# A prologue rewritten: filters by GpSimd's queue, one load for both middle matrices, x first, a shorter weight conversion

## The chip, the cores and the metric

The kernel runs on one core of a Trainium2 chip. The metric is the device time of one execution in microseconds, taken as the median of three runs. A profile of one execution shows every instruction of TensorE (PE), VectorE (DVE), ScalarE (ACT), GpSimd (POOL) and the queue of SyncE (SP), and every DMA packet.

## The reference

```
X = rfft(x, axis=1)                      # x: 8 x 3008 x 256, float32
y = irfft(X * (filt_r + 1j*filt_i), n=3008, axis=1)   # filters: 1505 x 256
t = y.reshape(24064, 256)
h = t @ w_in                             # 256 x 2048, stored as float64
out = (h - tanh(h)) @ w_out              # 2048 x 256, stored as float64
```

A circular convolution along the sequence comes first, then a feed-forward block with the activation h - tanh(h).

## The kernel before, in words

The length 3008 is 64 x 47, so each Fourier transform is done in two steps by matrix products. `first` applies the 64-point step to x and writes the result to the scratch tensor `ct1` in memory. `middle` reads `ct1` back (`load_a2`), applies the 47-point step with a matrix per frequency group (`f2`, giving `pz`), multiplies by the filters (`uv`, `zs`), applies the inverse 47-point step (`g3`, giving `pe`), and writes `ct2`. `last` reads `ct2` (`load_e2`), applies the inverse 64-point step and leaves the transposed tokens in `ut`. `up`, `shrink` and `down` are the feed-forward block, with seven products in place of eight blocks (the sums that this needs are GpSimd's `combine`). The batches are handled in five units: one batch, three pairs, one batch.

The first unit has a stage of its own, the prologue (L738 to L912). Nothing of the feed-forward block can run until its tokens are there, so it runs alone: `first0` for three pieces of x, then a loop over j = 0..15 with two frequencies each. Four frequencies (two values of j) share one load of `a2`, of the matrices and of the filters; the text calls such a group c, from 0 to 7. In this stage DVE computes `uv` and `zs` straight from PSUM (L899, L900), ACT copies the filters to the other 64 partitions (`double_filters`, L815) and builds `gx`, a turned copy of `g3` (`turned`, L823, L824), and `back0` makes `pe` and stores it to `ct2` (L879).

Beside it the weights are converted. They lie in memory as 64-bit floats and are loaded as pairs of 32-bit words (`raw`, L193, 512 KB a piece). `converted` turns one piece into float32 with integer operations on DVE and two on ACT (L200 to L219); every second piece is followed by four subtractions on GpSimd (L261 to L264) for the seven-product scheme. Ten pieces are converted in the prologue, six more (`late`) while the first unit's feed-forward block runs. In the same time the filters are copied from the inputs to the scratch tensor `filt_d` in the layout that the other units read (`filters_d`, 52 transfers from memory to memory, L791).

Order: in the prologue every instruction stands in the order of the program text, per engine. Transfers that are not part of it (the late weight pieces, the copies to `filt_d`) are put by the scheduler wherever it finds room on SP's queue. In the feed-forward stage PE, ACT, DVE and GpSimd are in the order of the text, with SP left to the scheduler. A queue works through its instructions in order, and one that waits holds up those behind it. The transfers that SP and ACT issue share eight completion counters in turn, so that an issue also waits until the transfer eight places earlier, on either queue, has landed; GpSimd's transfers have eight counters of their own.

Buffers of the prologue: `big` is a ring of five tiles of 8 KB a partition, used in turn by a tile of zeros, three pieces of x and the filters of each c; `a1` (three tiles) holds results of `first0`; the tiles of the conversion have rings of two.

Of the kernel before, what the change touches and what calls it, by code (L numbers as in the profile page):

```python
# [9 lines left out]
F32 = mybir.dt.float32  # L10
I32 = mybir.dt.int32
I64 = mybir.dt.int64
U8 = mybir.dt.uint8
AF = mybir.ActivationFunctionType
ALU = mybir.AluOpType
# [5 lines left out]
BATCH, SEQ, DM = 8, 3008, 256  # L21
NQ, NR = 64, 47
NK = NQ // 2
R2 = 2 * NR

RP = 48
RP2 = 2 * RP
LO = (NR + 1) // 2
HI = NR - LO
IM = 64  # L30
# [7 lines left out]
UNITS = [(0,), (1, 2), (3, 4), (5, 6), (7,)]  # L38
# [25 lines left out]
def _consts():  # L64
# [11 lines left out]
    wf1 = np.zeros((2, 128, 64, 2))  # L76
# [50 lines left out]
    for b in range(2):  # L127
        s2[64 * b:64 * b + 64, 64 * b:64 * b + 64] = s

    return [np.ascontiguousarray(v, dtype=np.float32) for v in (  # L130
        wf1,
        np.pad(f2w.transpose(1, 0, 2).reshape(R2, NK * 128), ((0, 2), (0, 0))),
        np.pad(g.transpose(1, 0, 2).reshape(IM + NR, NK, 2, NR),
               ((0, 1), (0, 0), (0, 0), (0, 1))).reshape(IM + RP, NK * RP2),
        s2)]


@with_exitstack
def kernel(
# [8 lines left out]
):  # L148
    nc = tc.nc
    V, G, ACT = nc.vector, nc.gpsimd, nc.scalar  # L150
    wf1_d, f2_d, g_d, s2_d = (
        nc.inline_tensor(v, name=n).ap() for v, n in zip(_consts(), ("wf1", "f2", "g", "s2")))


    ct1 = [nc.dram_tensor(f"ct1_{p}", (RP, 64 * len(bs), DM), F32, kind="Internal")
# [8 lines left out]
    def dram(t, off, dims):  # L164
        return bass.AP(tensor=t, offset=off, ap=[list(d) for d in dims])
# [21 lines left out]
    def converted(tiles, src, dsts, queue):  # L187

        n = src.shape[-1] * (src.shape[1] if len(src.shape) == 3 else 1)
        t = tiles("raw", I64, n)
        queue.dma_start(t if len(src.shape) == 2 else  # L193
                        t.rearrange("p (h n) -> p h n", h=src.shape[1]), src)
        yield
        words = t.bitcast(I32).rearrange("p (n w) -> p n w", w=2)
        lo, hi = words[:, :, 0], words[:, :, 1]
        it, lt, pt, st = (tiles(k, I32, n) for k in ("it", "lt", "pt", "st"))
        ft = tiles("ft", F32, n)
        V.tensor_scalar(out=it, in0=hi, scalar1=0xFFFFF, scalar2=None, op0=ALU.bitwise_and)  # L200
        ACT.activation(ft, it, AF.Identity, bias=1.0, scale=2.0 ** -20)

        V.tensor_scalar(out=pt, in0=hi, scalar1=20, scalar2=0x7FF,
                        op0=ALU.logical_shift_right, op1=ALU.bitwise_and)
        ACT.activation(pt, pt, AF.Relu, bias=exp_b)
        V.tensor_scalar(out=lt, in0=lo, scalar1=8, scalar2=None, op0=ALU.logical_shift_right)
        V.tensor_scalar(out=st, in0=hi, scalar1=-2 ** 31, scalar2=None, op0=ALU.bitwise_and)
        yield
        V.scalar_tensor_tensor(out=ft, in0=lt, scalar=2.0 ** -44, in1=ft,
                               op0=ALU.mult, op1=ALU.add)  # L210
        V.tensor_scalar_min(pt, pt, 255.0)
        V.scalar_tensor_tensor(out=pt, in0=pt, scalar=23, in1=st,
                               op0=ALU.logical_shift_left, op1=ALU.bitwise_or)
        pt = pt.bitcast(F32)
        for cols, dst, sign in dsts:
            f, p = ft[:, cols], pt[:, cols]
            if len(dst.shape) == 3:
                f, p = (v.rearrange("p (h n) -> p h n", h=dst.shape[1]) for v in (f, p))
            V.scalar_tensor_tensor(out=dst, in0=f, scalar=sign, in1=p, op0=ALU.mult, op1=ALU.mult)  # L219
        yield  # L220
# [46 lines left out]
    def halves(p, r, n):  # L267

        return [(h, slice(64 * h, 64 * h + 64), r + HALF * h, min(n, NR - r - HALF * h))
                for h in range(2) if r + HALF * h < NR]  # L270
# [42 lines left out]
                        a1[rows, 0:n_h, :])  # L313
            yield

    def load_slots(p, j):

        f2 = tr.tile([RP2, 4, 128], F32, tag="f2", bufs=2, name="f2")
        g3 = tr.tile([IM + RP, 4, RP2], F32, tag="g3", bufs=2, name="g3")
        nc.sync.dma_start(f2, f2_d[:, 4 * j * 128:4 * (j + 1) * 128])  # L320
        nc.sync.dma_start(g3, g_d[:, 4 * j * RP2:4 * (j + 1) * RP2])
        return f2, g3

    def load_a2(p, j, filters=True):

# [15 lines left out]
    def middle(p, z):  # L341
# [3 lines left out]
        n = NK // per  # L345
        w = BD // per
        a2 = {0: load_a2(p, 0)}
        mats = {0: load_slots(p, 0)}
        waiting = []
        yield  # L350

# [13 lines left out]
        for j in range(n):  # L365
# [1 line left out]
                a2[j // 2 + 1] = load_a2(p, j // 2 + 1)  # L367
            k4 = per * j // 4
            if per * j % 4 == 0 and k4 + 1 < NK // 4:
                mats[k4 + 1] = load_slots(p, k4 + 1)  # L370
            pz = z("pz", [128, per, w])
            at, ft = a2[j // 2] if j % 2 == 0 else a2.pop(j // 2)
            for i in range(per):
# [363 lines left out]
    with tc.tile_pool(name="tr", bufs=2) as tr:  # L737
        with tc.tile_pool(name="pro", bufs=1) as pro, \  # L738
# [2 lines left out]
            def z0(name, shape):  # L741
                return ps0.tile(shape, F32, tag="z", bufs=6, name=name)

            def big(shape, name):

                return pro.tile(shape, F32, tag="big", bufs=5, name=name)

            def load_x0(c):
                t = big([128, 8, DM], "x0")
                for _, rows, r, n in halves(0, 8 * c, 8):  # L750
                    nc.sync.dma_start(t[rows, 0:n, :],
                                      dram(x.tensor, r * DM, [[NR * DM, 64], [1, n * DM]]))
                return t

            def first0(xt, c):

                for i in range(2):
                    r = 8 * c + 4 * i
                    a1 = pro.tile([128, 4, DM], F32, tag="a1", bufs=3, name="a1")
                    parts = halves(0, r, 4)  # L760
                    m = parts[1][3]
                    for j in range(2):
# [17 lines left out]
            def filters_of(c, to=None):  # L780
# [4 lines left out]
                def put(row, m, v, i, n_s, src, off, dims):  # L785
                    if to is None:
                        dst = t[row:row + m, v, i:i + n_s, :]
                    else:
                        dst = dram(to, ((row * 2 + v) * NK + 4 * c + i) * DM,
                                   [[2 * NK * DM, m], [DM, n_s], [1, DM]])  # L790
                    nc.sync.dma_start(dst, dram(src.tensor, off, dims))  # L791

                if to is None:
                    t = big([128, 2, 4, DM], "filt")


                    G.memset(t[32:64], 0.0)
                    if n == 3:
                        G.memset(t[0:1, 1, 3], 0.0)
                for v, src in enumerate((filt_r, filt_i)):  # L800
# [23 lines left out]
                ACT.mul(t[IM:IM + RP], g3[0:RP], -1.0)  # L824

            def tiles0(k, dtype, n):
                return pro.tile([128, n], dtype, tag=k, bufs=3 if k == "raw" else 2, name=k)

            with tc.manual_schedule():
                nc.sync.dma_start(wf1, wf1_d)  # L830
                V.memset(near_b, B)
                V.memset(exp_b, -896.0)
                zero = big([128, 8 * DM], "zero")
                G.memset(zero, 0.0)
                gx = [pro.tile([IM + RP, 4, RP2], F32, name=f"gx{k}") for k in range(2)]
                for t in gx:
                    G.memset(t[32:64], 0.0)
                xs = [load_x0(0)]
                ws = weights(tiles0, range(5), 3)
                next(ws)  # L840
                xs += [load_x0(1), load_x0(2)]


                for p, bs in enumerate(UNITS):
                    G.dma_start(
                        dram(ct1[p], NR * 64 * len(bs) * DM, [[DM, 64 * len(bs)], [1, DM]]),
                        zero[0:64 * len(bs), 0:DM])
                row = 2 * NK * DM
                G.dma_start(dram(filt_d, RP * row, [[8 * DM, 128], [1, 8 * DM]]), zero)
                G.dma_start(dram(filt_d, NR * row, [[DM // 2, 128], [1, DM // 2]]),  # L850
                            zero[:, 0:DM // 2])
                G.dma_start(dram(filt_d, (NK + NK - 1) * DM, [[DM, 1], [1, DM]]), zero[0:1, 0:DM])
                G.dma_start(s2, s2_d)
                mats = {0: load_slots(0, 0)}
                fts = {0: filters_of(0)}
                for c in range(3):
                    for k, _ in enumerate(first0(xs[c], c)):
                        if k % 2 == 0:
                            next(ws)
                    if c == 0:  # L860
                        fts[1] = filters_of(1)
                a2 = {0: load_a2(0, 0, False)}
                double_filters(fts[0], 0)
                turned(mats[0][1], gx[0])
                waiting = []
# [16 lines left out]
                for j in range(NK // 2):  # L882
                    c = j // 2
                    if j % 2 == 0 and c + 1 < NK // 4:
                        a2[c + 1] = load_a2(0, c + 1, False)
                        mats[c + 1] = load_slots(0, c + 1)
                        if c + 2 < NK // 4:
                            fts[c + 2] = filters_of(c + 2)
                    pz = z0("pz", [128, 2, DM])
                    for i in range(2):  # L890
# [24 lines left out]
        with tc.tile_pool(name="dn", bufs=2) as dn, \  # L915
# [5 lines left out]

            def tiles1(k, dtype, n):

                tag = {"raw": "ft", "it": "uv", "lt": "zs", "pt": "a2", "st": "e1", "ft": "f2"}[k]
                return tr.tile([128, n], dtype, tag=tag, bufs=2, name=k)

            def filters_d():
                for c in range(NK // 4):
                    filters_of(c, filt_d)
                    yield  # L930
# [121 lines left out]
```

## Time and profile before

| | us |
|---|---|
| runs (median of three) | 2888.24 (2887.48 to 2889.82) |
| the profiled execution | 2892.35 |
| its span, first to last instruction | 2890.6 |
| prologue, to the first `pu` product | 129.4 |
| of it, to the first `pz` product | 48.7 |
| of it, the sixteen steps j, to the last `pe` | 73.0 |
| feed-forward block and other units | 2761 |

The profiled execution has 1.75 us outside its span. A page of the profile gives shares for the whole span; stages are read from busy time by window, waits by window and the order of instructions in time. In a list of waits, a line names the engine and line that waited, what released it, the total, the number of times and the longest.

### The profile page before, as it was taken

What the parts mean: (1) busy time and instruction counts of PE and PEld (TensorE: products, weight loads), DVE (VectorE), ACT (ScalarE), POOL (GpSimd) and SP (SyncE); (2) the same over time, 40 slices, a digit from 0 to 9 for tenths busy, and PEclk for the clock granted to TensorE, in tenths of its full rate; (3) what the DMA queues carried; (4) which work ended last, traced back from release to release, by engine and by line L of the source; (5) the groups of instructions that cost most, each with busy time, mean ns of one, the idle gap of its engine ahead of it and who ended that gap; (6) DMA issues with size and microseconds to landing.
All of it is one profiled execution on the core that took longest, in us unless ns stands there. A gap on an engine that the chain in (4) does not pass through costs nothing.

```text
span 2890.6 us, 36570 instructions
## 1 busy us (share of the span) xinstructions
PE 2746.8 (95%) x12474; PEld 2277.0 (79%) x12474; DVE 1998.8 (69%) x2230; ACT 1871.7 (65%) x2460; POOL 1736.7 (60%) x1338
## 2 busy tenths in 40 slices
PE   4789999999999999999999999999999999999996
PEld 2567777888878787888877887888888888888885
DVE  4585666766776677766776777767677767777765
ACT  4465666666667666666667766666666666666663
POOL 3245777544677767644576777654476666555544
PEclk8799999999999999999999999999999999999998
DMA  8655443233223322222223233312123222110100
GB/s 245 180 161 137 114 102 98 79 85 93 58 69 72 85 68 62 59 85 82 72 72 75 65 74 80 72 38 65 41 52 79 47 56 49 31 28 16 22 8 16
DMA packets 332377, 216.15 MB, mean 75 GB/s; under 512 B 229139, under 2 KB 285878, under 8 KB 331734
## 3 DMA queue, kind: packets, MB, share of 16 engines
q1 hardware_dynamic: 279316, 162.20, 23.4%
q10 hardware_dynamic: 52418, 49.82, 5.7%
q8 instruction: 100, 1.64, 0.2%
q0 software_dynamic: 448, 1.71, 0.1%
q14 instruction: 95, 0.78, 0.1%
HBM read 137.50 MB, written 79.17 MB: 75 GB/s over the span
## 4 chain that ended last, share of the span: by engine, by line
PE 66%; ACT 9%; DVE 9%; POOL 5%; issue 4%; DMA 4%; SPq 2%; ACTq 1%; DVEq 0%; POOLq 0%
PE o L576 26%; PE x L469 17%; PE z L469 7%; PE y L469 5%; PE pe L357 3%; DVE h L530 3%; PE pu L433 3%; ACT y L525 2%; PE pz L376 2%; PE pf L297 2%; ACT y L526 2%; SPq L633 1%; POOL t L451 1%; ACT u L475 1%; DVE h L505 1%
## 5 line engine op out<-in xcount | busy, mean ns | idle before, releaser
L576 PE MATMUL o<-t,wd 128*128 128x256 f32 (+2 forms) x3072 | 776.0, 375 | 1.8 <-POOL t L450 1.3
L530 DVE TENSOR_TENSOR h<-h,y 128x1024 f32<-128x1024 f32 (+2 forms) x384 | 590.2, 1537 | 252.9 <-ACT y L526 252.8
L448 POOL TENSOR_TENSOR t<-h 128x512 f32<-128x512 f32 (+2 forms) x192 | 240.6, 1253 | 743.3 <-DVE h L534 563.2
L576 PEld LDWEIGHTS o<-t,wd 128*128 128x128 f32 x3072 | 580.0, 190 | 74.4 <-POOL t L450 1.9
L469 PE MATMUL x<-tu,wu 128*128 128x256 f32 (+2 forms) x2304 | 588.8, 378 | 16.0 <-ACT u L475 15.0
L576 PE MATMUL o<-h,wd 128*128 128x256 f32 (+2 forms) x2304 | 581.3, 375 | 0.2 <-DVE h L534 0.2
L534 DVE SCALAR_TENSOR_TENSOR h<-sq,h 128x1024 f32<-128x1024 f32 (+2 forms) x384 | 566.5, 1475 | 21.5 <-DVE h L530 0.9
L469 PEld LDWEIGHTS x<-tu,wu 128*128 128x128 f32 x2304 | 428.1, 190 | 159.3 <-issue 73.4
L576 PEld LDWEIGHTS o<-h,wd 128*128 128x128 f32 x2304 | 430.7, 190 | 71.1 <-issue 18.3
L531 ACT ACTIVATE sq<-y,near_b 128x1024 f32<-128x1024 f32 (+2 forms) x384 | 435.4, 1134 | 5.6 <-DVE h L534 0.9
L525 ACT ACTIVATE y<-h 128x1024 f32<-128x1024 f32 (+2 forms) x384 | 400.0, 1042 | 14.8 <-ACT e L360 7.2
L475 ACT COPY s<-x 128x512 f32<-128x512 f32 (+2 forms) x192 | 110.7, 577 | 458.2 <-PE x L469 456.3
L526 ACT ACTIVATE y<-y 128x1024 f32<-128x1024 f32 (+2 forms) x384 | 399.2, 1040 | 12.1
L451 POOL TENSOR_TENSOR t<-t,h 128x512 f32<-128x512 f32 (+2 forms) x192 | 307.0, 1599 | 0.0
L475 ACT COPY u<-x 128x512 f32<-128x512 f32 (+2 forms) x384 | 219.2, 571 | 82.3 <-PE x L469 34.5
L449 POOL TENSOR_TENSOR t<-h,t 128x512 f32<-128x512 f32 (+2 forms) x192 | 241.1, 1256 | 15.1
L450 POOL TENSOR_TENSOR t<-h 128x512 f32<-128x512 f32 (+2 forms) x192 | 250.1, 1303 | 0.0
L392 POOL TENSOR_TENSOR zs<-zs,ft 128x512 f32<-128x512 f32 x112 | 168.0, 1500 | 135.9 <-ACT zs L390 135.8
L393 POOL TENSOR_TENSOR uv<-uv,zs 128x512 f32<-128x512 f32 x112 | 212.4, 1897 | 16.3 <-DVE uv L391 6.0
L469 PE MATMUL x<-ut,wu 128*128 128x256 f32 (+2 forms) x768 | 200.1, 383 | 14.5 <-DVE h L505 13.3
L485 DVE TENSOR_TENSOR h<-y,s 128x512 f32<-128x512 f32 (+2 forms) x192 | 130.3, 679 | 96.1 <-PE y L469 84.2
L469 PE MATMUL z<-tu,wu 128*128 128x256 f32 (+2 forms) x768 | 193.8, 375 | 2.1 <-DVE h L511 2.1
(104 smaller groups left out, 3308.3 us busy)
## 6 DMA issues: line engine op xcount, KB each, us to landing
a<-ct SPq DMA_DIRECT2D x64, 384.0 KB
ct<-e ACTq DMA_DIRECT2D x128, 192.0 KB
ft<-filt SPq DMA_DIRECT2D x96, 256.0 KB
out_dram<-ot SPq DMA_DIRECT2D x1408, 16.0 KB
ct<-a ACTq DMA_DIRECT2D x80, 256.0 KB
x_sb<-in_x_dram SPq DMA_DIRECT2D x69, 256.0 KB
e<-ct SPq DMA_DIRECT2D x33, 512.0 KB
ft<-filt SPq DMA_DIRECT2D x16, 512.0 KB
```

Of the source, the lines that this page charges most:

```text
L448: G.tensor_sub(t[0], b[0][1], b[0][0])
L449: G.tensor_sub(t[1], b[1][1], t[0])
L450: G.tensor_sub(t[2], b[1][1], b[0][1])
L451: G.tensor_sub(t[3], t[1], b[1][0])
L469: nc.tensor.matmul(bank[:, k], wu[:, q - 1, (2 * u + k) * 128:(2 * u + k + 1) * 128], rhs[q - 1], start=(first and k == 0), stop=True, ski ...
L475: ACT.copy(t, X)
L525: ACT.activation(y[k], ht[k], AF.Arctan, scale=S)
L526: ACT.activation(y[k], y[k], AF.Square)
L530: V.tensor_mul(ht[k], ht[k], y[k])
L531: ACT.activation(sq[k], y[k], AF.Square, bias=near_b, scale=A)
L534: V.scalar_tensor_tensor(out=ht[k], in0=sq[k], scalar=K, in1=ht[k], op0=ALU.add, op1=ALU.mult)
L576: nc.tensor.matmul(product(q), wd[:, q - 1, (2 * u + k) * 128: (2 * u + k + 1) * 128], rhs[q - 1][:, k], start=(u == 0 and k == 0 and q == ...
```

## The change: what it does

- The filters of the first batch are issued by GpSimd (L793 of the changed file) in place of SP, into three fixed tiles `filt` used in turn. The zero rows of each tile are written once, for the first three groups alone.
- `f2` and `g3` of a group lie side by side in one constant (`fg`), and one transfer loads both. In the prologue they go into the ring `a1`, now of four tiles, and are asked for two groups ahead; the first two groups' load is issued after that of `a2`.
- All three pieces of x are issued before the first piece of raw weights; the first piece of x in two cuts, so in four transfers.
- In the conversion the low word is taken unshifted, as an unsigned integer, with the factor 2^-52; the shift (`lt`, L206) is gone. The product that adds it (`ft`, L209) moves from the second to the first half of the conversion.
- The conversion's tiles in the prologue are quarters of one `big` tile; `big` has four tiles. The order of conversion halves within `first0` changes: two halves less in its steps.
- The tile of zeros and its eight transfers leave the start. Zeros for the first unit's `ct1` remain there (a `pad` of 64 x 256); the others are filled from a tile in the ring `a2` at the second unit of work of the feed-forward stage, by SP, in eight transfers.

```diff
@@ _consts
-        np.pad(f2w.transpose(1, 0, 2).reshape(R2, NK * 128), ((0, 2), (0, 0))),
...
+    fg = np.zeros((IM + RP, NK, 128 + RP2))
+    fg[:R2, :, :128] = f2w.transpose(1, 0, 2)
+    fg[:IM + NR, :, 128:].reshape(IM + NR, NK, 2, RP)[..., :NR] = \
+        g.transpose(1, 0, 2).reshape(IM + NR, NK, 2, NR)
@@ converted
-        it, lt, pt, st = (tiles(k, I32, n) for k in ("it", "lt", "pt", "st"))
+        lo, hi = words[:, :, 0].bitcast(U32), words[:, :, 1]
+        it, pt, st = (tiles(k, I32, n) for k in ("it", "pt", "st"))
...
-        V.tensor_scalar(out=lt, in0=lo, scalar1=8, scalar2=None, op0=ALU.logical_shift_right)
         V.tensor_scalar(out=st, in0=hi, scalar1=-2 ** 31, scalar2=None, op0=ALU.bitwise_and)
-        yield
-        V.scalar_tensor_tensor(out=ft, in0=lt, scalar=2.0 ** -44, in1=ft,
+        V.scalar_tensor_tensor(out=ft, in0=lo, scalar=2.0 ** -52, in1=ft,
                                op0=ALU.mult, op1=ALU.add)
+        yield
@@ load_slots
-        nc.sync.dma_start(f2, f2_d[:, 4 * j * 128:4 * (j + 1) * 128])
-        nc.sync.dma_start(g3, g_d[:, 4 * j * RP2:4 * (j + 1) * RP2])
+        nc.sync.dma_start(t, fg_d[:, w * j:w * (j + 1)])
+        return t[:, :, 0:128], t[:, :, 128:]
@@ prologue
-                nc.sync.dma_start(dst, dram(src.tensor, off, dims))
+                    (G if to is None else nc.sync).dma_start(dst, dram(src.tensor, off, dims))
                 if to is None:
-                    t = big([128, 2, 4, DM], "filt")
-                    G.memset(t[32:64], 0.0)
+                    t = filt[c % 3]
+                    if c < 3:
+                        G.memset(t[32:64], 0.0)
...
-                zero = big([128, 8 * DM], "zero")
-                G.memset(zero, 0.0)
-                xs = [load_x0(0)]
+                xs = [load_x0(0, (0, 4, 8))]
                 ws = weights(tiles0, range(5), 3)
-                next(ws)
                 xs += [load_x0(1), load_x0(2)]
-                for p, bs in enumerate(UNITS):
-                    G.dma_start(
-                        dram(ct1[p], NR * 64 * len(bs) * DM, [[DM, 64 * len(bs)], [1, DM]]),
-                        zero[0:64 * len(bs), 0:DM])
-                row = 2 * NK * DM
-                G.dma_start(dram(filt_d, RP * row, [[8 * DM, 128], [1, 8 * DM]]), zero)
...
+                pad = pro.tile([64, DM], F32, name="pad")
+                G.memset(pad, 0.0)
+                G.dma_start(dram(ct1[0], NR * 64 * DM, [[DM, 64], [1, DM]]), pad)
+                fts = {0: filters_of(0), 1: filters_of(1)}
...
+                next(ws)
                 for c in range(3):
                     for k, _ in enumerate(first0(xs[c], c)):
-                        if k % 2 == 0:
+                        if k == 3 or k == 1 and c > 0:
                             next(ws)
...
                 a2 = {0: load_a2(0, 0, False)}
+                mats = {0: load_slots(0, pro), 1: load_slots(1, pro)}
+                next(ws)
@@ loop over j
-                        mats[c + 1] = load_slots(0, c + 1)
                         if c + 2 < NK // 4:
+                            mats[c + 2] = load_slots(c + 2, pro)
                             fts[c + 2] = filters_of(c + 2)
@@ filters_d
+                zero = tr.tile([128, 4 * DM], F32, tag="a2", bufs=2, name="zero")
+                G.memset(zero, 0.0)
+                for p, bs in enumerate(UNITS[1:], 1):
+                    nc.sync.dma_start(
+                        dram(ct1[p], NR * 64 * len(bs) * DM, [[DM, 64 * len(bs)], [1, DM]]),
+                        zero[0:64 * len(bs), 0:DM])
+                yield
...
```

## The prediction

> **What bounds the kernel now.** First the page, for the span as a whole.
>
> ```profile
> PE 66%; ACT 9%; DVE 9%; POOL 5%; issue 4%; DMA 4%; SPq 2%; ACTq 1%; DVEq 0%; POOLq 0%
> PE   4789999999999999999999999999999999999996
> ```
>
> PE is full from the fifth slice (of 72 us) on and carries 66% of the chain that ended last. What the change touches lies in the first three slices: there PE has 4, 7 and 8 tenths. So time is to be had before about 230 us, and I read that stretch by stages, with the transfers of the first 50 us ahead.
>
> ```profile
> DMA packets 7290, 13.57 MB, mean 271 GB/s; under 512 B 809, under 2 KB 4580, under 8 KB 6842
> 48.70:122.00 73.30, 54.48 (x192) 38.23 (x192) 56.08 (x100) 38.89 (x58) 22.09 (x22) 0.83 0.70 195
> 134.00:232.00 98.00, 83.17 (x313) 60.29 (x313) 73.54 (x99) 60.46 (x83) 41.78 (x35) 0.94 0.51 154
> ```
>
> The columns of the windows are length, busy PE, PEld, DVE, ACT, POOL, PE's clock, DMA share, GB/s. Up to 48.7 us transfers bound: 271 GB/s at a share over 0.9 in most slices. From 48.7 to 122 nothing is full: PE 54 and DVE 56 of 73 us, transfers 195 GB/s. Something is waited for; the waits in that window and SP's own say what.
>
> ```profile
> PE pz L892 <- DMA f<-f: 15.6, 6, 6.0
> POOL wu L261 <- DVE wu L219: 43.9, 3, 24.3
> SPq L791 <- DMA ct<-e: 19.8, 6, 5.7
> SPq L751 <- DMA raw<-in_moe_w_in_dram: 7.6, 1, 7.6
> ```
>
> PE waits for the matrices, 15.6 us; SP, which loads them, sits 19.8 us in front of a filter load until stores of results (`ct<-e`) have landed. That is the eight counters: twelve transfers go out per group (six filters, `f`, `g`, `a`, `raw`, two `ct<-e`), so a load for the next group cannot leave before this group's stores have. In order of time:
>
> ```profile
> 67.06 6.92 SPq L791 DMA_DIRECT2D filt<-in_filt_r_dram  x3
> 75.99 0.41 SPq L328 DMA_DIRECT2D a<-ct  x1
> 76.45 0.41 SPq L320 DMA_DIRECT2D f<-f  x1
> 72.25 1.10 PE L892 MATMUL pz<-a,f 94*128 94x256 f32 x4 [2.90 <-DMA f<-f]
> 82.14 1.10 PE L892 MATMUL pz<-a,f 94*128 94x256 f32 x4 [2.78 <-DMA f<-f]
> 76.09 3.99 POOL L797 MEMSET filt<- 32x2048 f32 x2
> 76.23 2.10 DVE L206 TENSOR_SCALAR lt<-raw 128x512 int32<-128x512 int32 x1
> ```
>
> `f` leaves at 76.45 and PE starts on it at 82.14. Below: beside a GpSimd memset a 0.42 us DVE shift takes 2.10.
>
> **The change part by part**, against the span of 2890.6 us (run 2892.35; the median, 2888.24, is 4.1 lower).
>
> *To the first `pz`, 48.7 us.* The zeros leave (1.6 of 1.71 MB). But the built program's order on SP shows what the diff doesn't: with SP emptier, the scheduler puts two late weight pieces (1.05 MB) and nine copies to `filt_d` (0.56 MB) ahead of the first `a2`, and `fg` for group 0 (0.4 MB) now stands behind it. Needed by then: x and `wf1` 3.2, six raw pieces 3.1, late 1.05, copies 0.56, filters 1.13, pads 0.13, `ct1` 3.08, `a2` 0.39, `fg` 0.4: 13.1 MB against 13.27 landed at 48.7 before. A tie at one rate. For earlier: x is in by about 16 us (3.2 MB, and 0.8 MB of filters from the other queue, at 271 GB/s from 1.2 us on) instead of 21.8. Against: ACT has the first conversion's two operations between the second and third of its six pieces of `first0`, and raw lands at about 20 instead of 10, so ACT idles from 11 to 20. Then come four pieces of 2.5 us (two copies of 0.58, two issues of 0.65) and two conversions of 1.3: the last `ct1` store leaves at about 33 instead of 36.2. I take -2 us; bounds -6 (a2 issued at 38 instead of 41.1, half a megabyte less ahead of it) and +3 (0.8 MB at 271 GB/s).
>
> *The loop, 73.0 us, 9.1 a group.* Out go six filter issues and one matrix issue a group on SP; seven transfers share the counters in most groups (a, fg, raw, two stores, one or two copies) instead of twelve, and `fg` is asked for two groups ahead, so the 15.6 us of waits for `f` should go. What is late next, per group: PE, two `pz` of 1.03 and two times four `pe` pairs of 0.6: 6.9 us. ACT: doubling 1.99, `gx` 1.03, two stores with their copies 2.0, conversion 1.34, 6.3. DVE: `uv`, `zs` 4 x 0.68, conversion 3 x 0.42 + 0.68 + 0.42 + 0.69 + 0.76, 6.5 us; and as `ft` now stands in the first half, DVE waits there for ACT's product (0.63, behind a 0.58 copy), about 1.3: 7.8. The shift (0.42) is gone already in this count, and so are the memsets beside which four DVE operations of 0.42 took 1.71 to 2.10. Transfers: 15.0 MB (14.3 before, plus 28 copies of 1.75, less the two late pieces): at 271 GB/s 55 us, 6.9 a group. So DVE is next at 7.8; I take 8.2, with one 3 us lateness in eight groups. 8 x 8.2 = 65.6: -7.4 us. Bounds: -14 (7.35, between PE and DVE) and 0 (each `f` wait replaced by one for a filter).
>
> The moved work on POOL: six issues a group by the row of its memory transfers,
>
> ```profile
> 6.20 0.56 POOL L849 DMA_DIRECT2D filt<-zero  x1
> s_sb<-s POOLq DMA_DIRECT2D x1, 64.0 KB, 5.6
> filt<-zero POOLq DMA_DIRECT2D x1, 1024.0 KB, 9.4
> ```
>
> 3.4 us, landing 5.6 to 9.4 later. Tiles are three, so group c+3 waits until ACT and DVE are through with c; queued behind are the four subtractions (3.1 us in every second group), for which nobody waits before the feed-forward stage. Cover: two groups less the 3 us in which ACT doubles them, 2P - 3, must hold 3.1 + 3.4 + landing. At P = 8.2 that leaves 6.9 us for landing: covered by the 64 KB row, not by the 1 MB row. The pieces are 28 to 96 KB, so I take it as covered.
>
> [...]
>
> *To the first `pu`, 7.7 us* (`ct<-e` 2.13, `e<-ct` 4.24). 18 copies stand on SP after the last `a2`, 0.75 each, 13.5 us, beside two groups (16 us). +1 us; 0 to +4.
>
> *Feed-forward stage to 232 us.* Five shifts sum to 3.2 us there (four of 0.41 or 0.42, one of 1.52), the long one in the stretch where DVE is full (176 to 196: 19.65 of 20). Of the copies 15 of 52 remain instead of 47, so this goes too:
>
> ```profile
> 225.66 4.65 DMA x_sb<-in_x_dram
> ```
>
> an x piece issued behind copies, PE idle 3.05. In come eight zero transfers (1.5 MB, about 4 us) and a wait: the fourth late conversion's `ft` on ACT needs the tile of zeros back. ACT asks for it at 169.9 before; the memset can start at 153.6, the transfers land by about 162: hidden by 8 us; without that cover up to 4 us, for `up`'s copies behind it. Moving `ft` costs nothing here where DVE idles after it (2.48 and 1.74 us). Sum -3.6; bounds -8 and +2. The later units lose 32 SP issues; PE is full, 0.
>
> Sum: -2 - 7.4 + 1 - 3.6 = -12. Span 2878.6; on the median 2876.2.
>
> **The rivals.**
> 1. *No change: transfers bound the loop.* If 195 GB/s is what this mix carries, 15.0 MB take 77 us: +3.7 instead of -7.4, total -0.9: 2887. For: 37 copies from memory to memory now stand before `e2`, five before. Against: 271 GB/s in the first 50 us, and the waits show loads issued late, not slow.
> 2. *Slower: the filters come late.* The three tiles close a loop on POOL. If an issue takes 1.1 us (DVE's operations in between, half of the 2.10 row) and landing 9.4, 2P = 3 + 3.1 + 6.6 + 9.4, P = 11: +15 in place of -7.4, total +10.4: 2898.6. Decides once issue and landing exceed 13.3 us (P = 9.7) against the 9.0 taken.
> 3. *The scheduler's order gives it back at the start:* first `pz` late by 3 and the copies delay `e2` by 4: -7.4 + 7 - 3.6 = -4, 2884.
>
> **How the numbers follow.** Forecast 0.52 (faster 0.48, same 0.04), rival 1 0.16 (same), rival 2 0.2 (slower), rival 3 0.12 (faster 0.05, same 0.06, slower 0.01). Within 0.2% (5.8 us, about what a measurement of this kernel tells from no change): 0.26; faster 0.53, slower 0.21. Range: from 2864 (most of the -14 and -8 bounds) to 2898 (most of rival 2); the forecast's own is 2866 to 2884.
>
> **What would show it.** `PE pz <- DMA` near zero in the loop and groups near 8.2 us: right. A wait of ACT's L818 or DVE's `uv` for a GpSimd filter transfer, POOL's L793 over 1 us: rival 2. PE waiting for `fg` or `a`, with a DMA share above 0.85: rival 1. First `pz` outside 43 to 52, or `pu` later than 129: the start is wrong. Any gain behind 232 us is none of mine.

## The result, and the profile after

| | kernel before | changed kernel |
|---|---|---|
| median of six runs | 2888.06 us (2887.17 to 2892.93) | 2881.18 us (2878.37 to 2884.77) |
| the profiled execution | 2892.35 us | 2879.68 us |
| its span | 2890.6 us | 2877.8 us |

The ratio is 0.9975, with a 95% interval of 0.9962 to 0.9987: faster by a quarter of a per cent. Run again beside the last experiments it was 0.9958 (0.9945 to 0.9972), 2883.73 us against 2893.74. Predicted were 2876.2 us, 5 us below the median, in a range of 2864 to 2898.

The two profiled executions differ by 12.8 us of span and the medians by 6.9: the first lies 4.3 us above its median, the second 1.5 below its own. So the stages below are read with the repeats beside them. The page of the changed kernel, the two lines shown of before:

```profile
PE   4789999999999999999999999999999999999996
PE 66%; ACT 9%; DVE 9%; POOL 5%; DMA 4%; issue 4%; SPq 2%; ACTq 1%; DVEq 0%; POOLq 0%
```

Both read as before; a change worth 12 us does not show in slices of 72. The transfers up to the first `pz`, and the windows of the loop and of the feed-forward stage (columns as in the prediction):

```profile
DMA packets 7799, 13.87 MB, mean 251 GB/s; under 512 B 1042, under 2 KB 4454, under 8 KB 7607
```

```profile
55.20:120.70 65.50, 52.64 (x192) 34.87 (x192) 47.57 (x92) 39.80 (x60) 30.85 (x51) 0.90 0.83 220
134.00:232.00 98.00, 87.15 (x344) 64.20 (x343) 76.26 (x102) 63.39 (x88) 40.89 (x37) 0.97 0.60 187
```

By these windows the loop now takes 65.5 us instead of 73.3, at 220 GB/s instead of 195; counted to the start of the last eviction of `e`, as the loop is counted from here on, it takes 64.9 instead of 73.0. But it begins at 55.2 us instead of 48.7. The waits from there to 121 us:

```profile
PE pz L892 <- DMA fg<-fg: 14.5, 1, 14.5
ACT e L878 <- DMA ct<-e: 13.7, 5, 6.0
PE pz L892 <- DMA a<-ct: 4.2, 2, 3.5
```

The first line is the wait for the very first `pz`, which ends the start; inside the loop TensorE no longer waits for matrices. What came instead is the second line: ScalarE cannot evict the next `e` before an earlier store has landed.

By stages, each from one profile, in us (the last two columns are cut at fixed products of TensorE, the 801st, near 290 us, and the 12001st, near 2760 us):

| kernel | first `pz` | to first `pu` | to product 801 | to 12001 | to the end |
|---|---|---|---|---|---|
| before | 48.7 | 80.7 | 165.1 | 2474.9 | 121.2 |
| changed | 55.2 | 72.7 | 157.3 | 2473.1 | 119.5 |
| difference | +6.5 | -8.0 | -7.8 | -1.8 | -1.7 |
| changed, again | 53.6 | 72.5 | 157.7 | 2473.8 | 124.2 |
| one shift more | 53.5 | 70.5 | 158.0 | 2473.3 | 124.8 |

The last two have the same order of transfers as the changed kernel, so they show what one profile is worth: 2 us in each of the first two stages, 0.7 in the third, 5 in the last. The loss at the start, the gain in the loop and the gain behind it stand well out of that; the last column doesn't. The 1.8 us to product 12001 is more than the 0.7 by which the three profiles of that order differ there, but it is not the change's alone (see the later units below).

### The profile page after: what moved, and what is told of

It is laid out like the page before. It is cut to its first block, busy times and chain, and to the rows that moved or that the text cites. A ratio compares the mean times of both kernels' runs of the same rounds, so it can differ in the third digit from the quotient of the medians.

```text
span 2877.8 us, 36472 instructions
## 1 busy us (share of the span) xinstructions
PE 2740.2 (95%) x12474; PEld 2270.3 (79%) x12474; DVE 1984.1 (69%) x2214; ACT 1871.1 (65%) x2460; POOL 1748.9 (61%) x1379
## 4 chain that ended last, share of the span: by engine, by line
PE 66%; ACT 9%; DVE 9%; POOL 5%; DMA 4%; issue 4%; SPq 2%; ACTq 1%; DVEq 0%; POOLq 0%
PE o L577 26%; PE x L470 17%; PE z L470 7%; PE y L470 5%; PE pe L358 3%; DVE h L531 3%; PE pu L434 3%; PE pz L377 2%; ACT y L526 2%; PE pf L298 2%; ACT y L527 1%; SPq L634 1%; ACT u L476 1%; POOL t L452 1%; DMA ct<-e 1%
```

## The experiments: the start

**1. The conversions behind x.** In the changed kernel ScalarE, and SyncE in front of the first `a`, show this order in time:

```profile
12.62 12.27 SPq L195 DMA_DIRECT2D raw<-in_moe_w_in_dram  x3
25.43 0.63 ACT L203 ACTIVATE conv<-conv 128x512 f32<-128x512 int32 x1 [12.40 <-DVE conv L202]
38.72 0.86 ACT L773 COPY a<-pf 128x512 f32<-128x512 f32 x2 [4.74 <-DMA filt<-in_filt_i_dram]
41.18 2.60 ACTq L777 DMA_DIRECT2D ct<-a  x2
47.38 0.36 SPq L329 DMA_DIRECT2D a<-ct  x1
47.84 0.83 SPq L322 DMA_DIRECT2D fg<-fg  x2
```

The three raw pieces need 12.27 us to be issued: the first two wait for the counters of x transfers, the third, until 24.3 us, for that of a store of `ct1` which ScalarE issued at 10.6. The first piece lands at 25.0, and ScalarE sits 12.40 us in front of the first conversion step. Later it sits 4.74; the line names a copy moved ahead, but by the trace's semaphores 3.2 us of that are a wait for ScalarE's own store of 28.3 us, which landed at 37.2, and the rest is the issue of two more stores. The last store of `ct1` leaves at 43.2 us, and `a` and `fg` leave from 47.4 on.

```diff
                 for c in range(3):
-                    for k, _ in enumerate(first0(xs[c], c)):
-                        if k == 3 or k == 1 and c > 0:
-                            next(ws)
+                    for _ in first0(xs[c], c):
+                        pass
+                for _ in range(5):
+                    next(ws)
```

> The first three conversions' ScalarE and VectorE steps stand behind all of x's eviction instead of between its pieces; nothing else moves. Theory A (ScalarE, in its fixed order, waits for the raw weights that now land behind x, and the stores of ct1 leave late): the 12.4 us of idle time ahead of the first conversion step on ScalarE are gone, the last store of ct1 leaves by about 36 us instead of 43.2, and the first `pz` starts at 46 to 50 us instead of 55.2; the median falls by 4 to 7 us, to about 2875. Theory B (about 14 MB have to land by then whatever the order, and the store's own 6 to 9 us in the backlog set the end): the first `pz` stays at 53 us or later and the median within 2 us of 2881.

Measured: ratio 0.9982 (0.9972 to 0.9992), first `pz` at 56.9 us. By that number theory A falls; but the timeline shows that its first half came true:

```profile
36.14 1.25 ACTq L777 DMA_DIRECT2D ct<-a  x2
47.48 0.58 SPq L195 DMA_DIRECT2D raw<-in_moe_w_in_dram  x1
48.16 0.54 SPq L329 DMA_DIRECT2D a<-ct  x1
```

The last stores left 6 us earlier. Then SyncE stood at a raw load whose buffer the third conversion, now late, gave back at 47.4, with `a` queued behind it. One in-order wait had taken the place of the other. The bytes that land ahead of `pz` were the same but for half a megabyte, and in the ten microseconds in front of `a` they did not bind:

```profile
38.00:48.00 10.00, 0.00 (x0) 0.00 (x0) 9.74 (x18) 5.04 (x8) 3.44 (x5) 0.50 0.59 178
```

The DMA share there is 0.59; in the changed kernel it is 0.85 from 38.0 to 47.4 us. So here it was the wait that held `a`.

**2. `fg` ahead.**

```diff
                 next(ws)
+                mats = {0: load_slots(0), 1: load_slots(1)}
                 for c in range(3):
...
-                mats = {0: load_slots(0, pro), 1: load_slots(1, pro)}
```

> The first two `fg` tiles take the two `fg` slots of the later pool, which are free, and are issued behind the raw loads, so they no longer stand behind the first `a` on SyncE. Theory A (the wait of 14.5 us for `fg` was the last one by 2 us or less, because `a` was issued 0.46 us earlier into the same backlog): first `pz` at 53 to 55 us, waiting for `a` instead; median within 2 us of 2881. Theory B (`fg` alone was late): first `pz` at 50 to 52 us, median 2877.

Measured: 0.9964 (0.9950 to 0.9978), first `pz` at 53.0 us, waiting for `a`. As theory A has it; and with 53.5 and 53.6 in the repeats it is no gain at all. The 14.5 us of waiting for `fg` were named after the later of two transfers that left half a microsecond apart.

**3. The conversions behind the first `a`.** As 1, but the six steps stand behind the loads of `a` and `fg`:

```diff
                 for c in range(3):
-                    for k, _ in enumerate(first0(xs[c], c)):
-                        if k == 3 or k == 1 and c > 0:
-                            next(ws)
+                    for _ in first0(xs[c], c):
+                        pass
                 G.dma_start(s2, s2_d)
                 a2 = {0: load_a2(0, 0, False)}
                 mats = {0: load_slots(0, pro), 1: load_slots(1, pro)}
-                next(ws)
+                for _ in range(6):
+                    next(ws)
```

> As in the run with the conversions behind x, but their six steps, and with them the fourth to sixth raw load, now also stand behind the first `a` and the first two `fg` loads on SyncE. Theory A (a wait of one in-order engine turned into a wait of another: ScalarE for the raw weights, or, with that gone, SyncE for a free raw buffer in front of `a`): `a` leaves SyncE at 39 to 42 us instead of 47.4, first `pz` at 46 to 50 us instead of 55.2; the three conversions then stand in the loop, on a VectorE that has 2 to 3 us of each group free, and take back 0 to 4 us of it; first `pu` at 120 to 125 us instead of 127.9. Theory B (the bytes set the end): first `pz` at 53 us or later.

Measured: 0.9960 (0.9946 to 0.9974); first `pz` at 45.6 us, first `pu` at 121.1.

```profile
39.76 0.36 SPq L329 DMA_DIRECT2D a<-ct  x1
41.11 6.58 SPq L195 DMA_DIRECT2D raw<-in_moe_w_in_dram  x3
```

The 6.58 us in which the raw loads wait for buffers now lie behind `a`, and the numbers are those of theory A (`pz` 0.4 us earlier still). But the edit took more than a wait out: three raw pieces now land behind the first `pz`. Up to it, in this run and, for comparison, in experiment 1:

```profile
DMA packets 6667, 11.61 MB, mean 255 GB/s; under 512 B 850, under 2 KB 4234, under 8 KB 6475
```

```profile
DMA packets 7564, 13.39 MB, mean 235 GB/s; under 512 B 926, under 2 KB 4338, under 8 KB 7372
```

Against the changed kernel's 13.87 MB that is 2.26 MB less, at 253 GB/s 8.9 of the 9.6 us gained. So theory B was wrong in taking the bytes as given: the order decides which bytes stand ahead of `a`. Whether the gain is these bytes or the wait is not shown. For the wait speaks that `a` leaves 7.6 us earlier; for the bytes, that in the changed kernel the DMA share is 0.85 from 30 us on and 0.94 behind the issue of `a`. Experiment 1 does not part the two, since it put one wait in the place of another, and a run that takes out the bytes and leaves the wait was not made.

## The experiments: the loop

**4. The loop's filters by SyncE again.**

```diff
-                    (G if to is None else nc.sync).dma_start(dst, dram(src.tensor, off, dims))
+                    (G if to is None and c < 2 else nc.sync).dma_start(dst, dram(src.tensor, off, dims))
```

> The filters of the loop, from the third group on, go by SyncE's queue again; the first two groups stay on GpSimd, the three buffers and the single `fg` load stay. With SyncE busy with them, the program's order of the copies to the filter scratch changes too: none instead of 10 between the `a` loads, 8 instead of 18 from there to the first `e` load, 35 instead of 15 behind it. Theory A (the queue is what shortened the loop): from the first `pz` to the last eviction of `e` 72 to 74 us instead of 65, and `f`-like waits of TensorE for `fg` or `a` of 10 us or more. Theory B (three buffers and fewer loads did it, or the bytes): 63 to 67 us. Apart from that: if copies that stand ahead of `x` on SyncE make the wait of TensorE for `x_sb` at 230 us, the 35 copies bring it back (2 to 5 us, with one half-speed clock stretch behind it); if not, TensorE stays busy from 220 to 240 us.

Measured: 0.9988 (0.9978 to 0.9997); the loop takes 72.5 us, as under theory A. In it SyncE and TensorE wait as before the change, though for `a`, not for the matrices:

```profile
SPq L793 <- DMA ct<-e: 17.0, 5, 5.7
PE pz L892 <- DMA a<-ct: 9.3, 3, 5.0
```

The wait for `x_sb` did not come back. With 35 copies behind the first `e` load instead of 15, SyncE had at most six of them in a row between two loads of x; before there were ten. Their number is not what counts (experiment 6).

**5. GpSimd's queue alone, and the lead of `fg`.** First the kernel before with that edit only, then the changed kernel with `fg` asked for one group ahead:

```diff
# the kernel before
-                    nc.sync.dma_start(dst, dram(src.tensor, off, dims))
+                    (G if to is None else nc.sync).dma_start(dst, dram(src.tensor, off, dims))
# the changed kernel
-                mats = {0: load_slots(0, pro), 1: load_slots(1, pro)}
+                mats = {0: load_slots(0, pro)}
...
+                        mats[c + 1] = load_slots(c + 1, pro)
                         if c + 2 < NK // 4:
-                            mats[c + 2] = load_slots(c + 2, pro)
```

> The kernel before with one edit: the batch's filters go by GpSimd's queue, into the five rotating buffers as before; 42 of the 52 copies, which find SyncE free, then move ahead of the first `e` load (5 were). Theory A (the queue alone shortens the loop; three fixed buffers and the single load of the two matrices add nothing): the loop takes 64 to 67 us instead of 73.0. Theory B (the queue needs the other two edits): 70 us or more. First `pz`: 48 to 54 us, as the filters now stand behind the zeros on GpSimd's queue and the copies ahead of `a` on SyncE.

> The changed kernel, but the tile of both middle matrices for a group is asked for one group ahead, as `f2` and `g3` were before, not two. Theory A (GpSimd's queue alone left the loop at 69.4 us, with TensorE waiting 11.0 us for `f`; the second group of lead is the rest of the gain): the loop takes 68 to 71 us instead of 62 to 65, and TensorE waits for `fg` inside the loop. Theory B (the rest comes from the fixed filter buffers or from the single load): loop within 62 to 66 us, no wait for `fg` in it.

Measured: 69.4 us of loop in the first, between the ranges of its two theories (ratio 1.0007, 0.9996 to 1.0018), 68.5 in the second (0.9982, 0.9973 to 0.9992). The waits of the first, then of the second, which includes the 14.5 us ahead of the first `pz`:

```profile
PE pz L892 <- DMA f<-f: 11.0, 2, 6.3
```

```profile
PE pz L892 <- DMA fg<-fg: 24.2, 3, 14.5
```

Both keep some 10 us of waits for the matrices. So the gain of 8 us needs the queue (without it nothing is left) and the second group of lead (without it about half is left). What the fixed filter buffers and the single load add by themselves was not tried; at 69.4 and 68.5 us there is little room for it. In the first, 42 copies moved ahead of the first `e` load (5 in the kernel before, 37 in the changed kernel), and two late weight pieces ahead of the first `a`: it is the filters' leaving SyncE that lets them. Its first `pz` came at 55.4 us instead of 48.7, with the zeros still in place; 15.06 MB had landed by then, at 272 GB/s.

## The experiments: behind the loop

**6. The kernel before with its copies by GpSimd.**

```diff
-                    nc.sync.dma_start(dst, dram(src.tensor, off, dims))
+                    (nc.sync if to is None else G).dma_start(dst, dram(src.tensor, off, dims))
```

> The kernel before with one edit: its 52 copies to the filter scratch go by GpSimd's queue instead of SyncE's. Theory A (the wait of 3.0 us for `x_sb` at 230 us, and the half-speed clock stretch of 3.4 us behind it, came from the run of ten copies on SyncE between two loads of `x`, 214.8 to 225.3 us): TensorE waits for `x_sb` no more and the feed-forward phase up to 250 us is 4 to 6 us shorter; first `pz` and the loop within 1 us of 48.7 and 73.0, since only 5 copies stood ahead of the first `e` load; ratio to the kernel before 0.998 to 0.9985. Theory B (the wait comes from the zeros, or from the loads of `x` themselves): it stays, ratio 1.000.

Measured: 0.9995 (0.9985 to 1.0006). First the windows of the kernel before and then of this one:

```profile
228.00:234.00 6.00, 3.55 (x7) 2.25 (x8) 1.05 (x2) 2.09 (x4) 0.00 (x0) 0.72 0.70 177
```

```profile
220.00:240.00 20.00, 19.95 (x83) 15.37 (x82) 11.57 (x16) 12.68 (x19) 10.72 (x15) 1.00 0.50 153
```

Before, TensorE is idle for 2.5 of the 6 us and its granted clock falls to a mean of 0.72, which is half speed for 3.4 of them. With the copies off SyncE it is busy throughout at full clock, and the stretch from product 501 to 601 takes 24.1 us instead of 29.0, as in every run of this study but the kernel before. So the copies in a row caused the wait. The total did not follow: from the first `pz` to the first `pu` took 2.9 us longer, and from there to product 501 1.7 more. In the second of these stretches TensorE is at half speed for 6.8 us twice, where before it was for 3.4 twice. What set that off, and how much of the 2.9 is GpSimd's issues and how much the 2 us by which that stage moves anyhow, one profile does not say.

**7. One shift more** in each conversion, its result unused:

```diff
+        V.tensor_scalar(out=st, in0=words[:, :, 0], scalar1=8, scalar2=None,
+                        op0=ALU.logical_shift_right)
         V.tensor_scalar(out=st, in0=hi, scalar1=-2 ** 31, scalar2=None, op0=ALU.bitwise_and)
```

> The changed kernel with the shift of the lower words put back into each conversion (its result is not used). Theory A (the prediction's: five shifts of 0.6 us on VectorE in the feed-forward phase lie on the path): from the first `pu` to 250 us 2 to 4 us longer, ratio to the kernel before 0.9985. Theory B (VectorE has slack there; the shift lies beside other work): within 0.5 us, ratio 0.9975; the loop within 1 us of 64.9 in both.

Measured: 0.9971 (0.9962 to 0.9981). From the first `pu` to product 801 158.0 us against 157.3 and 157.7: 0.3 to 0.7 us for five shifts of 0.4 to 1.5 us. The two profiles of the changed kernel differ by 0.4 themselves. So the shifts lie beside other work, as theory B says.

**8. The changed kernel again.**

> The changed kernel once more. If the stage times of one profile repeat, first `pz` is at 54 to 56 us, the loop 64 to 66 us, the first `pu` at 127 to 129 us; if the order of landing among queued transfers varies from run to run, as 53.5, 62.4 and 124.0 us in the run with one more shift suggest, they move by 2 to 4 us without any change. From the first `pu` to instruction 800 of TensorE 167 to 168 us either way. Ratio 0.9975.

Measured: 0.9958 (0.9945 to 0.9972); 53.6, 64.8 and 126.2 us. (The 167 us of the expectations are counted from a product among the last `pe`; the table counts from the first `pu`, ten microseconds later.) The windows near the end, of the changed kernel and of its repeat:

```profile
2800.00:2804.00 4.00, 4.00 (x23) 3.74 (x23) 2.58 (x4) 1.58 (x2) 0.00 (x0) 1.00 0.00 0
```

```profile
2800.00:2808.00 8.00, 8.00 (x30) 7.10 (x30) 2.61 (x4) 2.47 (x6) 0.00 (x0) 0.57 0.00 0
```

The same program, equally busy; in one execution the clock stays at 1.00 until TensorE's last products, in the other it is halved for 3.4 us at 2790 and for 6.8 at 2801 (a mean of 0.57 over these 8 us). Half of 10.2 is 5.1 us; the ends differ by 4.7, the spans by 4.1.

## The experiments: a faster version

**9. The copies by GpSimd in the changed kernel.**

```diff
-                    (G if to is None else nc.sync).dma_start(dst, dram(src.tensor, off, dims))
+                    G.dma_start(dst, dram(src.tensor, off, dims))
```

> All 52 copies of filters to the scratch go by GpSimd's queue, at the places where the program has them (the feed-forward phase); none of them is then ahead of the first `e` load (37 were). Theory A (the copies' bytes, some 0.06 MB each, slow the start and the loop, which run at 200 to 240 GB/s): first `pz` 2 to 3 us earlier (9 copies, 0.56 MB), the loop 3 to 6 us shorter (28 copies, 1.7 MB, part of it beside chains that do not wait for bytes), and TensorE never waits for `x_sb`; GpSimd's 52 issues of about 0.55 us lie in its idle time; median 2871 to 2876. Theory B (the copies fill gaps only): first `pz` and loop within 1 us, median within 2 us of 2881. Theory C: GpSimd, busy 60% of the feed-forward phase, delivers `t` later by its 29 us of issues spread over some ten units; TensorE waits for `t`, 2885 or more.

Measured: 0.9979 (0.9968 to 0.9989); first `pz` at 52.7, 71.8 us to the first `pu`, 158.3 to product 801. Against the repeats that is nothing that one can tell from no change. For the start it is inconclusive: by the first `pz` 13.90 MB had landed, no less than in the changed kernel, as two later `fg` tiles moved ahead where the copies left. For the loop it says more:

```profile
52.70:117.10 64.40, 52.47 (x192) 35.82 (x192) 46.98 (x92) 40.19 (x60) 30.90 (x51) 0.88 0.77 199
```

The loop moves 12.83 MB instead of 14.42, and takes 64.4 us where by the same count the changed kernel took 65.5 and 65.4, and the run with one shift more 63.0. Theory A had 3 to 6 us for it. So the copies' bytes do not set the changed kernel's loop.

**10. Experiment 3 with four buffers for `e`, and 11. with 9 on top.**

```diff
-                    e1 = tr.tile([RP2, 2, DM], F32, tag="e1", bufs=2, name="e1")
+                    e1 = tr.tile([RP2, 2, DM], F32, tag=("e1", "fg")[j % 2], bufs=2, name="e1")
```

> The run with the conversions behind the first `a`, with four buffers for `e` in the loop instead of two (every other one in the later pool's free `fg` slots). Theory A (in that run ScalarE's wait for the store of `e`, 11.0 us in 4 waits, is the wait for a free `e` buffer while a store takes up to 9.65 us to land): the wait falls below 3 us and the loop from 67.8 to 61 to 65 us; first `pu` at 115 to 118 us. Theory B (it is the completion counter that the store shares with the loads on SyncE, or the bytes): the wait stays and the loop is 66 us or more. Ratio to the kernel before 0.994 under A, 0.996 under B.

> As that, and the 52 copies to the filter scratch by GpSimd's queue at their places in the program, so that none moves ahead of the first `e` load. Theory A (16 copies, 1 MB, in start and loop, and 19 behind the last `a`, take room from transfers that are waited for): first `pu` 2 to 4 us earlier than without, feed-forward the same. Theory B (what start and loop gain, GpSimd's issues take back, as 167.8 us from first `pu` to instruction 800 against 167.5 and one more half-speed stretch at 501 us hint): within 1 us of the run without.

Measured: 0.9945 (0.9931 to 0.9959) and 0.9931 (0.9918 to 0.9945). Loops of experiments 3, 10 and 11:

```profile
45.60:114.00 68.40, 56.31 (x192) 37.28 (x192) 51.28 (x98) 42.02 (x63) 38.05 (x61) 0.84 0.89 243
```

```profile
46.60:114.50 67.90, 55.10 (x192) 37.60 (x192) 50.69 (x99) 42.26 (x63) 38.23 (x61) 0.84 0.92 242
```

```profile
44.50:107.10 62.60, 55.08 (x192) 37.09 (x192) 51.07 (x98) 41.23 (x62) 37.74 (x60) 0.83 0.90 238
```

With four buffers ScalarE's 11.0 us of waits in front of `e` are gone, and the loop is as long as before (67.4 us against 67.8). Experiment 10 has another wait in their place, and experiment 11 has none such:

```profile
ACT filt L818 <- DMA ct<-e: 6.7, 1, 6.7
```

By the trace's semaphores this is the issue of a store of `e`, at 93.7 us, which waits for the counter of an earlier store, issued at 81.2 and landed at 93.7. So the wait for a buffer went, as theory A has it, and a wait for a counter, theory B's, stood behind it. The last column of the windows has a second candidate, the bytes. Multiplied by the windows' lengths it gives 16.6, 16.4 and 14.9 MB, all at about 240 GB/s and a DMA share of 0.89 to 0.92; only the third, which moves some 1.6 MB less, is shorter. Which of the two set these loops is not shown, since taking the copies off SyncE took out both the bytes and the wait. In the changed kernel's loop, at a share of 0.83, the same bytes were worth about 1 us (experiment 9). First `pu` at 115.0 us instead of 122.1, where theory A of the last run had 2 to 4 us for it.

The last version beats both kernels. In the same set of runs it took 2874.15 us (2871.86 to 2877.30), the changed kernel 2883.73 (2880.01 to 2884.14), the kernel before 2893.74.

## Why the prediction was right, and where it was wrong

**To the first `pz`: wrong.** Predicted -2 us, with bounds of -6 and +3; measured +6.5, and +4.9 in the repeat. The step that failed is "a tie at one rate": 13.1 MB against 13.27 before, both at 271 GB/s. It was 13.87 MB, 0.6 more than before, and 251 GB/s instead of 273: 2.3 us for the one (at 251) and 4.2 for the other. The path to it failed as well: the last store of `ct1`, put at about 33 us, left at 43.2. The windows from 10 to 20 us show where the rate went, before and after:

```profile
10.00:20.00 10.00, 5.84 (x8) 2.02 (x6) 5.64 (x13) 3.46 (x6) 4.86 (x3) 0.93 1.05 353
```

```profile
10.00:20.00 10.00, 6.40 (x11) 2.40 (x10) 0.00 (x0) 1.64 (x3) 2.99 (x6) 0.83 1.03 212
```

The DMA engines are full in both, at a share of 1.05 and 1.03. Before, these 10 us held most of the 1.6 MB of zeros, writes from one tile, beside the loads; after, loads and little else. Without the zeros the kernel before moved 11.7 MB in 48.7 us, 240 GB/s. So bytes that cost little were given up for 1.6 MB of late weights and copies, moved ahead. The first kernel of experiment 5 supports this: with the zeros kept and the late pieces and copies moved ahead, its first `pz` came at 55.4 us, as late as without the zeros. So it is the filters' leaving SyncE that costs the start, by what it lets ahead; whether through bytes or through waits was not parted (experiment 3). The first raw piece, put at about 20 us, landed at 25.0, and ScalarE idled until 25.4; what this wait costs by itself is open, since experiment 1 put another in its place.

**The loop: right, for half of the reason.** Predicted -7.4 (65.6 us); measured -8.1 (64.9), 64.8 in the repeat. That the waits for `f` would go is confirmed, and experiments 4 and 5 show that both things named for it, SyncE's six issues and the second group of lead, are needed. "DVE is next at 7.8" is not: VectorE is busy 47.6 of 65.5 us, 5.9 a group, and its waits for ScalarE's product come to 6.8 us in all. Nor are the copies' bytes next (experiment 9). What sets the loop now was not found; TensorE itself is busy 52.6 of the 65.5 us.

**The filters by GpSimd: right.** Issue 3.4 us for six and landing of 5.6 to 9.4 were taken from far rows. Measured in the loop:

```profile
L793 POOL DMA_DIRECT2D filt<-in_filt_r_dram x17: 517/532/774, 66.6 to 103.0; - x17
L793 POOL DMA_DIRECT2D filt<-in_filt_i_dram x17: 507/529/655, 68.5 to 106.5; - x17
DMA to landing us min/median/max: 3.2/6.3/9.9
```

Six times 0.53 is 3.2 us, and the median landing makes 9.5 with it against the 9.0 taken; rival 2 needed 13.3. The longest of the 34 issues was 0.77 us, beside a VectorE busy for 47.6 of the 65.5 us, where rival 2 took 1.1.

**To the first `pu`: right.** Predicted +1 (0 to +4), measured +0.1 (7.8 us from the last eviction of `e`). The 18 copies went out beside the last two groups.

**Feed-forward stage: the right cause, too small.** Predicted -3.6, of it 3.05 for the wait for x; measured -7.8 to product 801, inside the bounds of -8 and +2. The wait was worth 4.9 (experiment 6), because its 3.05 us were followed by 3.4 at half clock, which cost about half of that, 1.7 by estimate. The 0.55 left for the shifts fits experiment 7, which gives no more than the profiles differ by. Another half-speed stretch before the change, near 200 us, makes 1.7 more; what set it off was not traced. The zeros stayed hidden, as predicted.

**The later units.** Predicted 0; the profiles differ by 3.5 us there, 1.7 of it one half-speed stretch at the end, which experiment 8 puts down to the execution, not to the program. The other 1.8 was not traced; the kernel before with its filters by GpSimd (experiment 5) takes 2473.8 us to product 12001, as the changed kernel does.

So the sum, -12, came close to the two profiles' -12.8 by luck, through errors of opposite sign: a start 8.5 us worse than foreseen, 4.2 us more gain behind the loop than foreseen, 3.5 of gain in units where nothing was foreseen. The medians' -6.9, and -10.0 beside the last experiments, are the better measure.

**The rivals.** Rival 1 (195 GB/s is what the mix carries) is refuted: 220 to 243 GB/s were reached. Bytes may bind the loops of experiments 3 and 10, at about 240 GB/s; in the changed kernel's loop, at 220, 1.6 MB less brought about 1 us (experiment 9). Rival 2 was not seen. Rival 3 had the place right, with 3 us for the start where 5 to 6.5 were lost, and the delay of `e2` wrong; its 2884 lies 3 us above the median, as the forecast lies 5 below.

## What to carry to other kernels

Where transfers fill a stage, list what the built order puts ahead of the load that ends it, both the bytes and what its queue waits for: here 2.3 MB and a wait moved behind the first `a` brought the first `pz` 9.6 us forward, while letting stores leave 6 us earlier brought nothing, because another wait took the place of the first. A queue that is relieved fills up again: what left SyncE made room for late weights and copies that nobody needed yet, and the first `pz` came 5 to 7 us later. And when a wait goes, look for the one that stood behind it, as with the four buffers of `e`.

## What was not expected of the hardware

Near the end of the program the granted clock of TensorE falls to one half for stretches of 3.4 us, or twice that, and this makes steps in the time: the end, from product 12001 on, took 119.3 to 119.5, 121.1 to 121.8, or 123.9 to 125.1 us in the fourteen profiles, by no stretch there, one of 3.4, or two of 3.4 and 6.8 us. In the repeat shown eight products of 256 columns took 3.65 us in the first of the two stretches, against 1.96 in the first profile of the changed kernel. TensorE had not been idle for more than 0.4 us at a time from 2764 us until either stretch; each began about the end of 32 products of 48 columns (2786.7 to 2790.5 and 2797.6 to 2802.0 us), but in that first profile the same products ran and the clock stayed. What sets the stretches off was not found.
